# Two early reorderings in the attention stage: the third pair's key rest moves up GpSimd's queue, the fourth pair's copies move behind a reciprocal of the second pair

## The chip, the cores and the metric

One core of a Trainium2 chip runs the whole program in one launch. The metric is the device time of one execution in microseconds (us); a kernel's time is the median of its runs. A profiled execution gives the trace that is read here.

## The reference

Three stages follow each other: causal attention over 2 batches and 12 heads, a dense layer with a squared ReLU, and a layer of 8 experts of which each token takes the best one.

```
scores = q @ k.T / 8                  # seq 448, head_dim 64, causal mask
attn = exp(scores - max) ; attn = attn / (sum(attn) + 1e-9)
x = attn @ v                          # -> [896, 768]
x = relu(x @ w_in)**2 @ w_out         # 768 -> 2048 -> 768
e = argmax(normalised(x) @ normalised(expert_emb).T / tau)
out = gate * (relu(x @ w1[e]) @ w2[e])   # per token, 768 -> 1024 -> 768
```

## The kernel before

Every float32 operand of a product is split into a rounded part (`kh`, `vh`, `pt` high) and the rest (`kl`, `vl`, `pt` low), and three products of the parts make one product. Two heads make a **pair** (`units`, 12 of them; `units[0]` is the first pair here, `units[3]` the fourth). The queries of a pair lie in seven **chunks** of 64, c = 0 to 6; both heads of a chunk fill 128 rows.

For one pair the work is, in this order:

- `s_prep`: the scaled query is rounded on ScalarE (`qs` high) and its rest made on VectorE (`qs` low, line 219). From the third pair on, SyncE then copies it with two DMAs into one of two buffers `q` that TensorE reads (line 230). VectorE rounds the key (`kh`, line 66), and `s_rest` makes its rest (`kl`, line 71) on GpSimd.
- `s_scores`: TensorE makes the scores of a chunk (line 266: high, rest, high), VectorE masks them and finds the maximum (line 276 and a read-out), ScalarE takes the exponential into `p` and sums it (line 279).
- `s_norm`: VectorE makes the reciprocals of the sums (`rs`, line 288), GpSimd multiplies `p` by them (line 292). It is called once for chunks 2, 0, 1, 3 and once for 6, 4, 5.
- `s_trans`: TensorE transposes the probabilities in four groups, **T0 to T3** (line 310, four transposes each). ScalarE rounds a group (`pt` high, line 64), VectorE makes its rest (`pt` low, line 71). T0 needs chunks 0 to 3, T1 chunks 4 to 6. The groups take turns in two PSUM buffers, so T2 waits until VectorE has made T0's rest, T3 waits for T1's, and the next pair's T0 for T2's.
- `s_pv`: TensorE multiplies with v (line 328); the sums go to `xhi` and `xlo`.

The order on TensorE is written out (`products`, `half_unit`): a loop over half pairs k makes scores of one pair, transposes of the pair before it and products with v of the pair before that. On the other engines a scheduler sets the order; `tc.issue_after(x)` and `behind(x)` keep an instruction behind x in it. They put no wait into the program by themselves: on one engine they fix the order in which it works.

Of the kernel before, what the change touches and what calls it, by code (L numbers as in the profile page):

```python
# [13 lines left out]
ALU = mybir.AluOpType  # L14
# [3 lines left out]
B, H, S, D = 2, 12, 448, 64  # L18
# [14 lines left out]
def f32(ap):  # L33
    return ap.bitcast(F32)
# [18 lines left out]
def build(tc, qkd, vd, w_in, w_out, emb, tau, wm, cst, out, dbg_y=None):  # L53
    nc = tc.nc
    V, A, G, T, DMA = nc.vector, nc.scalar, nc.gpsimd, nc.tensor, nc.sync
# [14 lines left out]
    def lo_of(eng, lo, x, hi):  # L70
        return eng.tensor_tensor(out=lo, in0=x, in1=hi, op=ALU.subtract)  # L71
# [63 lines left out]
    last = {}  # L135
# [5 lines left out]
    units = [(b, pr) for b in range(B) for pr in range(NP_)]  # L141
    NU = len(units)
# [6 lines left out]
    maskf = apool.tile([P, S], F32, name="maskf")  # L149
# [19 lines left out]
    def ab(key, u):  # L169
        x = CFG[key]  # L170
        return ENG[x[units.index(u) % len(x)]]
# [24 lines left out]
    def behind(ins):  # L196
        return nullcontext() if ins is None else tc.issue_after(ins.ins)
# [38 lines left out]

    def s_rest(u, eng):
        d = st[u]
        lo_of(eng, d["kl"], d["k"], f32(d["kh"]))

    def s_prep_v(u):
        d = st[u]
# [9 lines left out]
    def s_scores(u, c):  # L252

        d = st[u]
        if "p" not in d:
            for x in ("sm", "mn", "rs"):
                d[x] = apool.tile([P, NQ], F32, tag=x, bufs=3, name=x)
            d["p"] = pz[units.index(u) % len(pz)]
        n = (c + 1) * QC
        ss = ps_s.tile([P, 512], F32, tag="s", name="s")[:, 0:n]  # L260
        first = units.index(u) < CFG["pm"]
        i = COL[c]
        mn = d["mn"][:, i:i + 1]
        order = ((0, "kh"), (1, "kh"), (0, "kl")) if first else ((0, "kh"), (0, "kl"), (1, "kh"))
        for i_, (x, y) in enumerate(order):
            T.matmul(ss, d["q2"][:, c, :, :, x].rearrange("p a b -> p (a b)"), d[y][:, :n],  # L266
                     start=i_ == 0, stop=i_ == 2 and not first)
            if i_ < 2:
                yield
        if first:  # L270

            T.matmul(ss[:, n - QC:n], identb, mask, start=False, stop=True)
            last["max"] = V.reduce_max(out=mn, in_=ss, axis=AX.X, negate=True)
        else:

            last["max"] = V.tensor_tensor_reduce(out=ss, in0=ss, in1=maskf[:, S - n:], scale=-1.0, scalar=3.0e38,  # L276
                                                 op0=ALU.add, op1=ALU.min, accum_out=mn)
        last["max", units.index(u), c] = last["max"]
        last["exp", units.index(u), c] = A.activation(d["p"][c][:, :n], ss, AF.Exp, bias=mn,  # L279
                                                      scale=1.0 if first else -1.0, accum_out=d["sm"][:, i:i + 1])  # L280
        yield
# [95 lines left out]
    def norm_at(k):  # L377
        u = (k + 2) // 2
        if 0 <= u < NU:
            s_norm(units[u], sum(CFG["ch"][k % 2], ()))  # L380
            last["norm", k] = last["norm"]
# [26 lines left out]
    def half_unit(k):  # L408

        u, h = divmod(k, 2)  # L410
        run = {}
        for x in (6, 4, 5) if h == 0 else (2, 0, 1, 3):
            v = u + 1 + h
            if 0 <= v < NU:
                run["s", x] = s_scores(units[v], x)
        if 0 <= u < NU:
            for i in (0, 1) if h == 0 else (2, 3):
                run["t", i] = trans(units[u], i)
        if 1 <= u <= NU:
            for j, g in ((0, 1), (3, 1), (0, 0), (3, 0)) if h == 0 else ((1, 0), (2, 0), (1, 1), (2, 1)):  # L420
                run["v", j, g] = s_pv(units[u - 1], j, g)
        return run
# [56 lines left out]
    def products(k, run):  # L479

        h = k % 2
        if k > 20:
            return last_products(k, run)
        if h == 0:
            mix(run, ("s", 6))
            mix(run, ("t", 0))
            mix(run, ("v", 0, 1), ("v", 3, 1), ("v", 0, 0))
            mix(run, ("s", 4))
            mix(run, ("s", 5))
            mix(run, ("v", 3, 0))  # L490
            if k < 20:
                mix(run, ("t", 1))
            else:
                left.update(run)
        elif k == -3:
            mix(run, *(("s", c) for c in (2, 0, 1, 3)))
        else:
            mix(run, ("t", 2))
            mix(run, ("s", 2))
            mix(run, ("s", 0), ("v", 1, 0))  # L500
            mix(run, ("s", 1), ("v", 2, 0))
            mix(run, ("v", 1, 1))
            mix(run, ("v", 2, 1))
            mix(run, ("t", 3))
            mix(run, ("s", 3))

    for k in range(-3, 2 * NU + 2):
        u, h = divmod(k, 2)
        if k == -2:
            load_v(units[1], last["max", 0, 3])  # L510
            s_load(units[3], last["max", 0, 3])
        elif h == 0:
            if u + 4 < NU:
                with behind(last["q"]):
                    s_load(units[u + 4])
            if u + 2 < NU:
                load_v(units[u + 2])
        if k == 3:
            with tc.issue_after(last["load", 3].ins):
                DMA.dma_start(out=ct, in_=cst)  # L520
        while len(wt) < min(NWI, max(0, (k - CFG["conv0"]) // CFG["convs"])):
            if CFG["pin"]:
                with tc.issue_after(last["max"].ins):
                    w_in_load()
            else:
                w_in_load()
        norm_at(k)
        if k == -1:
            with tc.issue_after(last["norm"].ins):
                s_rest(units[2], ab("kl", units[2]))  # L530
        products(k, half_unit(k))
        if k == -3:
            s_prep(units[1], None, last["max", 0, 3])
            zero_p(1)
            zeros.__exit__(None, None, None)
        if k == 5:
            with behind(last["norm"]):
                G.memset(tri, 1.0)
                G.affine_select(out=tri, in_=tri, pattern=[[1, P]], compare_op=ALU.is_gt, fill=0.0, base=0,
                                channel_multiplier=-1)  # L540
        if k + 3 < len(CFG["wn"]):
            warm(CFG["wn"][k + 3])
        if h == 0 and u + 3 < NU:
            i = u + 1
            s_prep(units[u + 3], last["exp", i, 6 if i else 3], last["max", i, 5], last["max", i, 5], i > 0)
        if h == 1 and 0 <= u + 1 < NU:
            with (tc.issue_after(last["rcp"].ins), tc.issue_after(last["max", 0, 5].ins), tc.issue_after(last["exp", 0, 5].ins),
                  tc.issue_after(last["norm", max(k - 2, 0 if k > 0 else -1)].ins)):
                s_prep_v(units[u + 1])
# [970 lines left out]
```

## Time and profile before

| | us |
|---|---|
| median of 3 runs | 542.58 |
| the runs | 542.92, 542.58, 540.73 |
| profiled execution, its own time | 542.75 |
| its span from first to last instruction | 541.0 |
| TensorE busy in the span | 529.0 |
| VectorE, ScalarE, GpSimd busy | 413.3, 287.4, 201.1 |

The span is cut at the first and the last instruction, so it is 1.75 us shorter than the execution's own time. Times in the rows below count from the span's start. The attention stage lasts from about 5 to about 110 us; the change touches its first quarter.

### The profile page before, as it was taken

What the parts mean: (1) busy time and instruction counts of PE and PEld (TensorE: products, weight loads), DVE (VectorE), ACT (ScalarE), POOL (GpSimd) and SP (SyncE); (2) the same over time, 40 slices, a digit from 0 to 9 for tenths busy, and PEclk for the clock granted to TensorE, in tenths of its full rate; (3) what the DMA queues carried; (4) which work ended last, traced back from release to release, by engine and by line L of the source; (5) the groups of instructions that cost most, each with busy time, mean ns of one, the idle gap of its engine ahead of it and who ended that gap; (6) DMA issues with size and microseconds to landing.
All of it is one profiled execution on the core that took longest, in us unless ns stands there. A gap on an engine that the chain in (4) does not pass through costs nothing.

```text
span 541.0 us, 9614 instructions
## 1 busy us (share of the span) xinstructions
PE 529.0 (98%) x3373; PEld 498.6 (92%) x3374; DVE 413.3 (76%) x979; ACT 287.4 (53%) x635; POOL 201.1 (37%) x270
## 2 busy tenths in 40 slices
PE   8999999999999999999999999999999999999993
PEld 5899999999999999999999989999999999999992
DVE  6989989766786969597899776895296897983741
ACT  6898887333335242433332326631386887764651
POOL 6788989936545643231011201026201301400010
PEclk9999999999999999999999999999999999999998
DMA  4676584333446555358200019304968889884310
GB/s 158 174 184 146 146 238 126 119 115 94 142 138 212 164 186 175 121 174 273 80 30 30 21 31 410 153 2 134 353 210 264 270 278 371 265 277 156 119 53 6
DMA packets 28473, 89.22 MB, mean 165 GB/s; under 512 B 2926, under 2 KB 12270, under 8 KB 28416
## 3 DMA queue, kind: packets, MB, share of 16 engines
q1 hardware_dynamic: 26880, 82.23, 47.6%
q0 software_dynamic: 1536, 6.29, 3.1%
q8 instruction: 28, 0.46, 0.3%
q14 instruction: 29, 0.24, 0.1%
HBM read 78.39 MB, written 6.32 MB: 157 GB/s over the span
## 4 chain that ended last, share of the span: by engine, by line
PE 94%; DVE 3%; POOL 1%; ACT 1%; issue 0%; POOLq 0%; DVEq 0%; ACTq 0%
PE pa L355 22%; PE yps L709 20%; PE ops L1118 11%; PE pv L328 7%; PE s L266 6%; PE pt L310 4%; PE hps L1012 3%; PE ops L1044 3%; PE ops L1049 3%; PE hps L1030 2%; PE hps L1032 2%; PE hps L1031 2%; PE hps L1044 2%; PE hps L1049 2%; PE hps L1013 1%; DVE ml L71 1%
## 5 line engine op out<-in xcount | busy, mean ns | idle before, releaser
L71 DVE TENSOR_TENSOR ml<-xraw,mh 128x768 fp32r<-128x768 f32 x64 | 59.4, 954 | 9.8 <-ACT mh L64 9.4
L64 ACT ACTIVATE mh<-xraw 128x768 fp32r<-128x768 f32 x64 | 52.1, 843 | 7.2 <-PE ops L1044 5.8
L1118 PE MATMUL ops<-mh,act 128*128 128x384 f32 x224 | 53.5, 341 | 0.0
L279 ACT ACTIVATE p<-s,mn 128x192 f32<-128x192 f32 (+6 forms) x84 | 39.9, 478 | 13.8 <-DVE mn L276 7.4
L328 PE MATMUL pv<-pt,v 128*128 128x448 f32 (+7 forms) x288 | 46.2, 295 | 0.0
L266 PE MATMUL s<-kh,q 128*128 128x128 f32 (+6 forms) x168 | 45.6, 323 | 0.2 <-POOL maskf L393 0.2
L292 POOL TENSOR_SCALAR p<-p,rs 128x192 f32<-128x192 f32 (+6 forms) x84 | 43.9, 542 | 3.3 <-DVE rs L288 3.3
L129 DVE SCALAR_TENSOR_TENSOR w<-raw,w 128x768 int32<-128x768 int32 x32 | 42.7, 1338 | 0.7
L328 PEld LDWEIGHTS pv<-pt,v 128*128 128x128 f32 (+1 forms) x288 | 38.5, 163 | 1.9
L1118 PEld LDWEIGHTS ops<-mh,act 128*128 128x128 f32 x224 | 39.2, 188 | 0.8
L1144 POOL DMA_INDIRECT out<-osb,fsi x10 | 10.1, 1013 | 78.4 <-ACT osb L1139 48.8
L71 DVE TENSOR_TENSOR ml<-mraw,mh 128x768 fp32r<-128x768 f32 x32 | 30.1, 955 | 11.3 <-ACT mh L64 10.9
L125 DVE TENSOR_SCALAR w<-raw 128x768 int32<-128x768 int32 x32 | 23.2, 726 | 18.6 <-DMA raw<-in_w_in 4.7
L358 ACT ACTIVATE relu<-pa 128x448 f32<-128x448 f32 x32 | 17.2, 538 | 35.7 <-PE pa L355 35.6
L806 POOL CAST gh<-g 128x1 fp32r<-128x1 f32 x7 | 3.5, 504 | 87.7 <-DVE OHs L800 31.8
L127 DVE SCALAR_TENSOR_TENSOR w<-raw,w 128x768 int32<-128x768 int32 x32 | 35.5, 1113 | 0.7
L71 DVE TENSOR_TENSOR pt<-pt 128x512 fp32r<-128x512 f32 x48 | 32.6, 683 | 2.0 <-ACT pt L64 1.9
L266 PEld LDWEIGHTS s<-kh,q 128*128 128x128 f32 x168 | 31.7, 208 | 2.5 <-POOL maskf L393 1.0
L276 DVE CUSTOM_DVE_ANT_0 s<-s,maskf 128x192 f32<-128x192 f32 (+6 forms) x77 | 31.9, 429 | 2.6 <-PE s L266 2.4
L64 ACT ACTIVATE hs<-h 128x512 fp32r<-128x512 f32 (+1 forms) x32 | 17.7, 573 | 29.5 <-PE yps L709 27.5
L64 ACT ACTIVATE pt<-pt 128x512 fp32r<-128x512 f32 x48 | 28.3, 601 | 7.0 <-PE pt L310 7.0
L71 DVE TENSOR_TENSOR hs<-h,hs 128x512 fp32r<-128x512 f32 (+1 forms) x32 | 21.9, 689 | 13.1 <-ACT hs L64 12.9
(472 smaller groups left out, 1681.2 us busy)
## 6 DMA issues: line engine op xcount, KB each, us to landing
xraw<-in_wm SPq DMA_DIRECT2D x32, 768.0 KB, 5.5
raw<-in_w_in SPq DMA_DIRECT2D x16, 768.0 KB, 4.2
raw<-in_w_out SPq DMA_DIRECT2D x16, 768.0 KB, 4.3
mraw<-in_wm SPq DMA_DIRECT2D x16, 768.0 KB, 8.4
qk<-in_qkd SPq DMA_DIRECT2D x11, 448.0 KB, 4.7
q<-qs SPq DMA_DIRECT2D x20, 224.0 KB, 4.7
v<-in_vd SPq DMA_DIRECT2D x12, 256.0 KB, 5.1
eb<-edram SPq DMA_DIRECT2D x8, 384.0 KB, 4.4
```

Of the source, the lines that this page charges most:

```text
L64: return A.activation(out, in_, AF.Copy, scale=scale)
L71: return eng.tensor_tensor(out=lo, in0=x, in1=hi, op=ALU.subtract)
L127: V.scalar_tensor_tensor(out=w[:, x], in0=raw[:, x, 1], scalar=-0x40000000, in1=w[:, x], op0=ALU.bitwise_and, op1=ALU.bitwise_or)
L129: V.scalar_tensor_tensor(out=w[:, x], in0=raw[:, x, 0], scalar=29, in1=w[:, x], op0=ALU.logical_shift_right, op1=ALU.bitwise_or)
L266: T.matmul(ss, d["q2"][:, c, :, :, x].rearrange("p a b -> p (a b)"), d[y][:, :n], start=i_ == 0, stop=i_ == 2 and not first)
L276: last["max"] = V.tensor_tensor_reduce(out=ss, in0=ss, in1=maskf[:, S - n:], scale=-1.0, scalar=3.0e38, op0=ALU.add, op1=ALU.min, accum_ou ...
L279: last["exp", units.index(u), c] = A.activation(d["p"][c][:, :n], ss, AF.Exp, bias=mn, scale=1.0 if first else -1.0, accum_out=d["sm"][:, ...
L292: last["norm"] = G.tensor_scalar(out=p, in0=p, scalar1=rs[:, COL[c]:COL[c] + 1], scalar2=1.0, op0=ALU.mult, op1=ALU.mult)
L328: T.matmul(d["pv"][:, j * P:S] if h else d["pv"][0:D, j * P:S], d[x][:, j, 1:3].rearrange("p a b -> p (a b)") if h else d[x][:, j, 0], pt[ ...
L355: T.matmul(ps, w[:, kc * P:(kc + 1) * P], x[:, kc, gs], start=n == 1, stop=n == 3 * KC)
L709: T.matmul(ps[t][c][:, :384], x, w[:, c * 384:(c + 1) * 384], start=(f == 0 and w is wh and x is hi), stop=(f == NF - 1 and x is lo))
L1118: T.matmul(ps[c], x, ww[:, col[c]], start=(fc == 0 and x is hh and ww is wh), stop=(fc == 7 and x is hl))
```

## The change

Four edits. At k = -1 the second normalisation of the first pair (chunks 6, 4, 5) is kept behind the third pair's `kl` on GpSimd, where `kl` was behind it or free. The maximum of the second pair's chunk 3 is kept behind the reciprocal of that normalisation on VectorE. The fourth pair's `s_prep` is called at k = 1 in place of k = 0, its rounded query behind the exponential of the second pair's chunk 5, its query rest and rounded key behind the second pair's second reciprocal. The fourth pair's `kl` is kept behind the second pair's last normalisation on GpSimd.

```diff
     def s_rest(u, eng):
         d = st[u]
-        lo_of(eng, d["kl"], d["k"], f32(d["kh"]))
+        last["kl"] = lo_of(eng, d["kl"], d["k"], f32(d["kh"]))
...
-            last["max"] = V.tensor_tensor_reduce(out=ss, in0=ss, in1=maskf[:, S - n:], scale=-1.0, scalar=3.0e38,
-                                                 op0=ALU.add, op1=ALU.min, accum_out=mn)
+            with behind(last["rcp"] if (units.index(u), c) == (1, 3) else None):
+                last["max"] = V.tensor_tensor_reduce(out=ss, in0=ss, in1=maskf[:, S - n:], scale=-1.0, scalar=3.0e38,
+                                                     op0=ALU.add, op1=ALU.min, accum_out=mn)
...
-        norm_at(k)
         if k == -1:
             with tc.issue_after(last["norm"].ins):
                 s_rest(units[2], ab("kl", units[2]))
+            with tc.issue_after(last["kl"].ins):
+                norm_at(k)
+        else:
+            norm_at(k)
...
+        if k == 1:
+            s_prep(units[3], last["exp", 1, 5], last["rcp"], last["rcp"], False)
+            with tc.issue_after(last["norm"].ins):
+                s_rest(units[3], ab("kl", units[3]))
-        if h == 0 and u + 3 < NU:
+        if h == 0 and u + 3 < NU and u != 0:
```

TensorE's own order is the same in both kernels. On the other engines the scheduler's order changes from here to the end of the attention stage; the three places below are the first.

On GpSimd, from the first pair's second normalisation on. `p0c` are the probabilities of the first and third pair, `p1c` of the second; `kl_258` is the third pair's key rest, `kl_347` (afterwards `kl_395`) the fourth pair's, `v10` the second pair's rounded v. Before:

```order
L292 TENSOR_SCALAR p06_121<-p06_121,rs_177 128x448
L292 TENSOR_SCALAR p04_119<-p04_119,rs_177 128x320
L292 TENSOR_SCALAR p05_120<-p05_120,rs_177 128x384
L71 TENSOR_TENSOR kl_258<-qk_155,kh_257 128x448
L292 TENSOR_SCALAR p12_124<-p12_124,rs_273 128x192
L292 TENSOR_SCALAR p10_122<-p10_122,rs_273 128x64
L292 TENSOR_SCALAR p11_123<-p11_123,rs_273 128x128
L292 TENSOR_SCALAR p13_125<-p13_125,rs_273 128x256
L66 CAST v10_113<-v_222 128x4x2x64
L71 TENSOR_TENSOR kl_347<-qk_225,kh_346 128x448
L292 TENSOR_SCALAR p16_128<-p16_128,rs_273 128x448
```

Now:

```order
L71 TENSOR_TENSOR kl_258<-qk_155,kh_257 128x448
L293 TENSOR_SCALAR p06_121<-p06_121,rs_177 128x448
L293 TENSOR_SCALAR p04_119<-p04_119,rs_177 128x320
L293 TENSOR_SCALAR p05_120<-p05_120,rs_177 128x384
L293 TENSOR_SCALAR p12_124<-p12_124,rs_273 128x192
L293 TENSOR_SCALAR p10_122<-p10_122,rs_273 128x64
L293 TENSOR_SCALAR p11_123<-p11_123,rs_273 128x128
L293 TENSOR_SCALAR p13_125<-p13_125,rs_273 128x256
L66 CAST v10_113<-v_222 128x4x2x64
L293 TENSOR_SCALAR p16_128<-p16_128,rs_273 128x448
L293 TENSOR_SCALAR p14_126<-p14_126,rs_273 128x320
L293 TENSOR_SCALAR p15_127<-p15_127,rs_273 128x384
```

The third pair's key rest stands one normalisation earlier; the fourth pair's is gone from this stretch and comes two rows after its end, behind the rest of the second pair's v.

On VectorE, behind the maximum of the second pair's chunk 5. `qs_348` (afterwards `qs_396`) and `kh_346` (`kh_394`) are the fourth pair's, `pt_319<-pt_339` is the rest of the first pair's T1, `pt_361<-pt_362` (afterwards `pt_352<-pt_353`) that of its T2; lines 276 and 277 (an `ISA` row and a read-out) are the maxima of the third pair. Before:

```order
L219 SCALAR_TENSOR_TENSOR qs_348<-qk_225,qs_348 128x448
L66 CAST kh_346<-qk_225 128x448
L276 ISA s_372,mn_370<-s_372,maskf_129 128x192
L276 ISA mn_370 128x1
L71 TENSOR_TENSOR pt_319<-pt_339,pt_318 128x512
L276 ISA s_378,mn_370<-s_378,maskf_129 128x64
L276 ISA mn_370 128x1
L276 ISA s_384,mn_370<-s_384,maskf_129 128x128
L276 ISA mn_370 128x1
L287 TENSOR_SCALAR rs_273<-sm_271 128x3
L71 TENSOR_TENSOR pt_361<-pt_362,pt_360 128x512
L288 RECIPROCAL rs_273<-rs_273 128x3
```

Now:

```order
L71 TENSOR_TENSOR pt_319<-pt_339,pt_318 128x512
L277 ISA s_363,mn_361<-s_363,maskf_129 128x192
L277 ISA mn_361 128x1
L288 TENSOR_SCALAR rs_273<-sm_271 128x3
L277 ISA s_369,mn_361<-s_369,maskf_129 128x64
L277 ISA mn_361 128x1
L277 ISA s_375,mn_361<-s_375,maskf_129 128x128
L277 ISA mn_361 128x1
L289 RECIPROCAL rs_273<-rs_273 128x3
L219 SCALAR_TENSOR_TENSOR qs_396<-qk_225,qs_396 128x448
L66 CAST kh_394<-qk_225 128x448
L71 TENSOR_TENSOR pt_352<-pt_353,pt_351 128x512
```

The fourth pair's two instructions moved from ahead of T1's rest to just ahead of T2's rest, and the reciprocal moved ahead of them.

On ScalarE, at the second pair's exponentials (`p16`, `p14`, `p15`). `pt_318<-pt_339` is the rounded T1 of the first pair, `qs` the fourth pair's rounded query. Before:

```order
L279 ACTIVATE p16_128,sm_271<-s_312,mn_272 128x448
L64 ACTIVATE qs_348<-qk_225 128x448
L279 ACTIVATE p14_126,sm_271<-s_327,mn_272 128x320
L64 ACTIVATE pt_318<-pt_339 128x512
L279 ACTIVATE p15_127,sm_271<-s_333,mn_272 128x384
```

Now:

```order
L280 ACTIVATE p16_128,sm_271<-s_312,mn_272 128x448
L280 ACTIVATE p14_126,sm_271<-s_327,mn_272 128x320
L64 ACTIVATE pt_318<-pt_339 128x512
L280 ACTIVATE p15_127,sm_271<-s_333,mn_272 128x384
L64 ACTIVATE qs_396<-qk_225 128x448
```

The rounded query moved behind the last of the three exponentials and behind T1's rounding.

## Rows read from the trace of the kernel before

**Rows 1.** The page's first part: busy us (share of the span) xinstructions

```profile
PE 529.0 (98%) x3373; PEld 498.6 (92%) x3374; DVE 413.3 (76%) x979; ACT 287.4 (53%) x635; POOL 201.1 (37%) x270
```

**Rows 2.** Busy time by stretch: stretch, us, each engine, clock, DMA share, GB/s

```profile
20.00:30.00 10.00, 9.22 (x76) 8.90 (x75) 9.17 (x34) 8.74 (x29) 8.81 (x16) 1.00 0.62 151
30.00:40.00 10.00, 10.00 (x79) 9.65 (x78) 9.04 (x30) 9.00 (x28) 8.28 (x16) 1.00 0.84 218
```

**Rows 3.** TensorE's waits, 0 to 60 us: us in total, times, longest

```profile
PE pt L310 <- DVE pt L71: 1.0, 2, 0.8
```

**Rows 4.** TensorE's timeline: start, us, instruction, count, [idle before, releaser]

```profile
18.08 0.89 PE L310 MATMUL pt<-ident,p 128*128 128x128 f32 x4
19.19 0.63 PE L310 MATMUL pt<-ident,p 128*128 128x128 f32 x4 [0.21 <-DVE pt L71]
19.57 0.34 PE L266 MATMUL s<-kh,q 128*128 128x192 f32 x1
...
20.55 0.28 PE L266 MATMUL s<-kh,q 128*128 128x128 f32 x1
21.62 0.63 PE L310 MATMUL pt<-ident,p 128*128 128x128 f32 x4 [0.78 <-DVE pt L71]
...
23.06 0.60 PE L310 MATMUL pt<-ident,p 128*128 128x128 f32 x4
...
26.86 0.34 PE L266 MATMUL s<-kh,q 128*128 128x192 f32 x1
...
45.76 0.75 PE L310 MATMUL pt<-ident,p 128*128 128x128 f32 x4
```

**Rows 5.** GpSimd's timeline, 16 to 26 us

```profile
16.38 1.99 POOL L292 TENSOR_SCALAR p<-p,rs 128x448 f32<-128x448 f32 x3 [2.35 <-DVE rs L288]
18.34 1.14 POOL L71 TENSOR_TENSOR kl<-qk,kh 128x448 fp32r<-128x448 f32 x1
19.46 2.10 POOL L292 TENSOR_SCALAR p<-p,rs 128x192 f32<-128x192 f32 x4
...
23.23 1.71 POOL L292 TENSOR_SCALAR p<-p,rs 128x448 f32<-128x448 f32 x3
24.90 1.29 POOL L71 TENSOR_TENSOR v<-v,v 128x512 fp32r<-128x512 f32 x1
```

**Rows 6.** VectorE's timeline, 14 to 23 us

```profile
14.62 0.39 DVE L66 CAST kh<-qk 128x448 fp32r<-128x448 f32 x1
...
16.04 0.17 DVE L288 RECIPROCAL rs<-rs 128x3 f32<-128x3 f32 x1
...
18.36 0.69 DVE L71 TENSOR_TENSOR pt<-pt 128x512 fp32r<-128x512 f32 x1
...
19.43 0.62 DVE L219 SCALAR_TENSOR_TENSOR qs<-qk,qs 128x448 fp32r<-128x448 f32 x1
19.98 0.61 DVE L66 CAST kh<-qk 128x448 fp32r<-128x448 f32 x1
...
20.79 0.68 DVE L71 TENSOR_TENSOR pt<-pt 128x512 fp32r<-128x512 f32 x1
...
22.06 0.68 DVE L71 TENSOR_TENSOR pt<-pt 128x512 fp32r<-128x512 f32 x1
```

**Rows 7.** ScalarE's timeline, 18 to 20 us

```profile
18.40 0.62 ACT L64 ACTIVATE qs<-qk 128x448 fp32r<-128x448 f32 x1
18.91 0.52 ACT L279 ACTIVATE p<-s,mn 128x320 f32<-128x320 f32 x1
...
19.41 0.60 ACT L64 ACTIVATE pt<-pt 128x512 fp32r<-128x512 f32 x1
```

**Rows 8.** SyncE's DMA issues: the query copies of the third and the fourth pair

```profile
14.79 1.37 SPq L230 DMA_DIRECT2D q<-qs  x2
...
20.13 1.39 SPq L230 DMA_DIRECT2D q<-qs  x2
```

**Rows 9.** Tile `qs`, 0 to 60 us: count, ns min/median/max, first and last start

```profile
L219 DVE SCALAR_TENSOR_TENSOR qs<-qk,qs x7: 616/624/1449, 14.1 to 57.0; 128x448 fp32r<-128x448 f32 x7
```

## The prediction

> **What bounds the kernel now.** I read the busy times first. TensorE is busy 529.0 of a span of 541.0 us [rows 1], and from 30 us on whole stretches of the attention stage are full, 10.00 of 10 us, at the full granted clock, the 2.4 GHz level [rows 2]. TensorE's instructions stand in the same order in both kernels, so the change can only give or take waits of TensorE. Next I read where it waits: up to 60 us the list shows 1.0 us behind VectorE's `pt` rests, in two waits [rows 3]. In TensorE's timeline [rows 4] they lie ahead of T2 (0.21 us) and T3 (0.78 us) of the first pair. A wait inside a group does not show as idle: T1 at 18.08 us lasts 0.89 us where the undisturbed T0 at 23.06 lasts 0.60, so 0.29 us is stretch. The next disturbed group of this kind that I show is T0 at 45.76, 0.75 us for 0.60. What the touched stretch could give back is thus little: 0.29 + 0.21 us around T1 and T2, and about 0.95 us ahead of T3 (from the last score matmul at 20.55 to T3 at 21.62 are 1.07 us, of which some 0.12 us is the distance of such matmuls). That is 1.45 us, 0.27% of the run, if all of it stays given back.
>
> **The third pair's key rest.** GpSimd was idle for 2.35 us before 16.38, that is from 14.03, waiting for the reciprocal [rows 5]. The rounded key is ready at 14.62 + 0.39 = 15.01 [rows 6], so `kl`, 1.14 us long [rows 5], fits into that gap and ends near 16.2. The reciprocal, at 16.04 before, now precedes one maximum and can start some 0.38 us earlier, at about 15.66 (an estimate: the three maxima around it leave no idle time). It ends at 15.83 with its 0.17 us; before, the normalisation followed its end (16.21) by 0.17, so 16.0 would be possible and `kl`'s end, 16.2, decides. The normalisation of chunks 6, 4, 5 then starts 0.18 us earlier and ends at 18.19 in place of 18.37. T1, which had to wait for it, ends near 18.8 instead of 18.97. But T2 did not wait for T1: it waited for VectorE's rest of T0 (18.36 + 0.69 = 19.05, released at 19.19) [rows 4, 6], and nothing ahead of that rest moves except the reciprocal among the maxima, which keeps the sum. T2 stays at 19.19 and this part gives **0**. The second pair's normalisation comes 1.14 us earlier, but the T0 that needs it ran undisturbed at 23.06 already.
>
> **The rest of T1 moves up.** Before, T1's rest was behind the fourth pair's query rest and rounded key (19.43 to about 20.5) and a maximum, and ran from 20.79 to 21.47; T3 followed at 21.62, 0.15 us later [rows 4, 6]. Now VectorE reaches it at 19.43, and what decides is T1's rounding on ScalarE. That stood at 19.41, behind the fourth pair's rounded query, which took 0.51 us of the queue (18.40 to 18.91) [rows 7]. So it now starts between 18.9 and 19.41; I take 19.1, since the exponential ahead of it needs a maximum that VectorE ends only just behind 18.36. With its 0.60 us the rest starts at 19.7 (bounds 19.5 and 20.04), ends at 20.4, and T3 could go at 20.55; TensorE gets there at 20.67. T3 gains **0.95 us** (0.74 if the rounding stays at 19.41).
>
> **Where that goes.** The next group, the second pair's T0, needs the buffer of T2, hence T2's rest on VectorE. It ran from 22.06 to 22.74, and T0 at 23.06 found it ready [rows 4, 6]. From 19.43 to 22.06 VectorE worked through eight things in 2.63 us: query rest, rounded key, three maxima, T1's rest, the sums' addition. Now it must go through the same ones and a reciprocal (0.17 us alone, about 0.09 in the queue) between the start of T1's rest and the start of T2's: 2.72 us. From 19.7 that makes 22.42; the rest then ends at 23.1, and T0 can start at 23.25 by the same release of 0.15 us. Two of the durations in the 2.63 us look stretched, above all the rounded key with 0.61 us where the third pair's took 0.39 [rows 6]; without that it is 23.0. The bounds: rest of T1 at 19.5 and 0.45 us less stretch (key and addition) give 22.6, and 20.04 gives 23.6. I take 23.15. So T3 runs a microsecond early and TensorE then waits for T2's rest instead: the wait moves by one group. Against 23.06 this is **+0.1 us**, bounds -0.45 and +0.55.
>
> **The fourth pair's copies.** Its query rest now ends about 0.5 us (key 0.4 to 0.6) ahead of T2's rest at 22.42, near 21.9, against 20.05 before. Issue followed by 0.08 us (20.13) [rows 6, 8], so now at 22.0. The third pair's copy was issued at 14.79, and TensorE used it at 19.57 without a wait [rows 4, 8], so 4.78 us from first issue to use is enough: 26.8. TensorE wants it at 26.86, or 0.1 later by the step above. Cost **0**, with almost no margin left by this bound, where there were 2 us. What is queued behind these DMAs on SyncE is the load of a pair needed a whole pair later. `kl` of the fourth pair: reciprocal near 21.3, normalisation about 0.34 us behind it as at 16.04 and 16.38, then 1.71, 1.29 for the rest of v and 1.14 for `kl` itself [rows 5, 6]: 25.8, which is 1 us ahead of its use.
>
> **The order after that.** VectorE, ScalarE and GpSimd keep a changed order up to the end of the stage, with the same instructions. TensorE is full there, so a better order can give back only stretches like that at 45.76 (0.15 us) [rows 4]; a worse one can add such a stretch to each of nine later pairs, up to 9 x 0.15 = 1.4 us. I take **0**.
>
> **A rule weighed.** The fourth pair's query rest took 0.62 us in the median of seven and 1.45 us at most [rows 9]: something can hold it for 0.8 us. The Trainium skill, "SBUF — State Buffer", section "Who interferes with whom", says that VectorE (with two SBUF inputs or in a two-port mode) and GpSimd exclude each other from a shared pair of ports for a whole instruction. The trace agrees in so far as the rounded key took 0.61 us beside GpSimd's four multiplies, and these 2.10 us [rows 5, 6]. By that rule the moved query rest would meet the second pair's second normalisation, which starts just behind the same reciprocal.
>
> **The sum.** The profiled execution took 542.75 us; 0 + 0.1 + 0 + 0 makes 542.85. It stands 0.17 us above the median of the runs, so I predict **542.6 us**: the same time.
>
> **Rivals.**
>
> - The gain stays. If T2's rest is ready by 22.2, T0 of the second pair starts up to 0.95 us early and all later work with it: 541.6; with the stretch of 45.76 gone, 541.5. For it: the stretches in the 2.63 us; against it: VectorE is busy 9.17 of 10 us there [rows 2] and has no idle time to give.
> - The query rest is held. In its new place, beside the second pair's second normalisation on GpSimd, it takes 1.45 instead of 0.62 us [rows 9], and T2's rest, the second pair's T0 and all behind it shift by 0.8 us: 543.4. For it: six of seven took about 0.62, one did not; against it: the rest would start ahead of the normalisation, which trailed the end of its reciprocal by 0.17 us. The rule weighed above speaks for this case.
> - On the slower side: the fourth pair's query lands late. Place: TensorE at 26.9, before the fourth pair's first scores; nothing else can fill in, since its order is fixed. From 4.9 us behind its issue at 22.0 on, every us costs one us; at 5.6 us the time is 543.3. To be slower by over 0.5% it would have to land after 29.6, 7.6 us behind its issue, for which no row speaks.
> - The later order adds its stretches: up to 542.6 + 1.4 = 544.0.
>
> **Chances and range.** Forecast (542.0 to 543.2) 0.55; the gain stays 0.20; the query rest held 0.08; the query late 0.05; later stretches 0.08; something later in the run that I do not see 0.04. A measurement of this kernel tells a change of about 0.5% from none, that is 2.7 us; no case reaches it, so faster has 0.05, slower 0.04, the same 0.91, where the first two hold the unseen and the width of the runs (2.2 us). The range covers the kept gain with the lower of the runs, 540.8, up to the later stretches, 544.0.
>
> **What would show it.** Right: T2 of the first pair at about 19.2, T3 near 20.7 without a wait, a new wait of TensorE for VectorE's `pt` ahead of the second pair's T0, that T0 near 23.1 and the fourth pair's first scores near 26.9; `kl` of the third pair on GpSimd from 15.05. Wrong: T0 at 22.1 to 22.5 (the gain stays), the scores of the fourth pair behind a wait for a DMA, or T0s of later pairs that last well over 0.60 us.

## The result, and the profile after

The changed kernel's median is 543.69 us (8 runs, 543.32 to 545.84) against 541.50 us (8 runs, 540.47 to 542.92) of the kernel before on the same chip: ratio 1.0051, 95% interval 1.0036 to 1.0067 (the quotient of the two medians alone is 1.0040). The time lies inside the predicted range, but "the same" had been forecast, and the changed kernel is slower by 0.5%: a ratio of 1 lies outside the interval. The runs of either kernel lie in two groups some 2 us apart, and the trace ahead of the prediction is one of the upper group, that of the changed kernel one of the lower; so from here on the changed kernel is compared with a second profile of the kernel before, of the lower group (execution 540.59 us, span 538.9).

The changed kernel's page, its stretches, and TensorE's waits up to 60 us (answering to [rows 1 to 3]):

```profile
PE 527.5 (97%) x3374; PEld 496.7 (92%) x3374; DVE 414.2 (76%) x979; ACT 287.4 (53%) x635; POOL 202.8 (37%) x270
```

```profile
20.00:30.00 10.00, 9.58 (x73) 8.82 (x73) 8.80 (x29) 8.77 (x30) 8.51 (x13) 1.00 0.84 185
30.00:40.00 10.00, 10.00 (x80) 9.68 (x80) 9.27 (x30) 8.56 (x27) 8.56 (x19) 1.00 0.63 160
40.00:50.00 10.00, 9.33 (x77) 8.83 (x75) 9.10 (x29) 8.89 (x27) 8.73 (x16) 1.00 0.57 144
```

```profile
PE pt L311 <- POOL p L293: 1.6, 4, 0.7
...
PE pt L311 <- DVE pt L71: 0.2, 1, 0.2
PE s L266 <- ACT p L280: 0.2, 1, 0.2
```

Where the transposes waited only for VectorE's `pt` rests [rows 3], four of their waits are now for GpSimd's probabilities, 1.6 us together. TensorE's timeline of the changed kernel, the first pair's T1, T2 and T3, the second pair's T0, and what stands behind (as [rows 4]):

```profile
16.66 0.33 PE L311 MATMUL pt<-ident,p 128*128 128x128 f32 x1 [0.68 <-POOL p L293]
17.23 0.99 PE L311 MATMUL pt<-ident,p 128*128 128x128 f32 x7 [0.23 <-POOL p L293]
...
19.19 0.66 PE L311 MATMUL pt<-ident,p 128*128 128x128 f32 x4
...
21.52 0.63 PE L311 MATMUL pt<-ident,p 128*128 128x128 f32 x4 [0.23 <-DVE pt L71]
...
25.33 0.34 PE L266 MATMUL s<-kh,q 128*128 128x192 f32 x1
```

```profile
47.80 0.33 PE L311 MATMUL pt<-ident,p 128*128 128x128 f32 x1 [0.43 <-POOL p L293]
48.36 0.98 PE L311 MATMUL pt<-ident,p 128*128 128x128 f32 x7 [0.24 <-POOL p L293]
```

```profile
104.19 0.31 PE L329 MATMUL pv<-pt,v 128*64 128x320 f32 x1
105.51 1.54 PE L329 MATMUL pv<-pt,v 128*64 128x320 f32 x11 [1.01 <-DVE pt L71]
```

TensorE's order is the same in both kernels, so the two traces can be laid over each other matmul by matmul. The **lag** of the changed kernel, that is how much later the same matmul starts than in the second profile of before, at the places where it changes:

```
before   after    lag
 14.37   14.41   +0.04   T0, first pair
 16.13   17.23   +1.10   T1, first pair (waits for GpSimd's p)
 19.31   19.19   -0.12   T3, first pair
 20.75   21.52   +0.76   T0, second pair
 46.69   48.36   +1.67   T1, fifth pair (waits for GpSimd's p)
 54.56   56.09   +1.52
 88.56   90.45   +1.89   scores (wait for ScalarE's p)
102.35  105.51   +3.16   last products with v (wait for VectorE's pt)
  end     end    +3.3    spans 538.9 and 542.2
```

So 0.8 us are lost where the change was made, and 2.5 us further on, at three places: 0.9, 0.4 and 1.3 us (about 0.2 us come back near 55 us). The two traces thus differ by 3.3 us; the ratio of the runs makes it 2.8 us (2.0 to 3.6). Behind the attention stage nothing changes: 436.55 us from that last place to the end before, 436.69 now.

GpSimd, VectorE and SyncE at the first place, of the changed kernel (as [rows 5, 6, 8]):

```profile
13.86 1.62 POOL L71 TENSOR_TENSOR kl<-qk,kh 128x448 fp32r<-128x448 f32 x1
15.46 3.21 POOL L293 TENSOR_SCALAR p<-p,rs 128x448 f32<-128x448 f32 x7
```

```profile
18.44 0.69 DVE L71 TENSOR_TENSOR pt<-pt 128x512 fp32r<-128x512 f32 x1 [1.21 <-ACT pt L64]
...
19.87 0.60 DVE L219 SCALAR_TENSOR_TENSOR qs<-qk,qs 128x448 fp32r<-128x448 f32 x1
20.39 0.39 DVE L66 CAST kh<-qk 128x448 fp32r<-128x448 f32 x1
20.69 0.68 DVE L71 TENSOR_TENSOR pt<-pt 128x512 fp32r<-128x512 f32 x1
```

```profile
20.54 1.28 SPq L230 DMA_DIRECT2D q<-qs  x2
```

T1's rest (18.44) waits for T1, T1 waits for the normalisation (15.46), and that for `kl`.

The second of the three places can be read from the traces at hand: it lies in ScalarE's order near 90 us. Of the kernel before (second profile), then of the changed one, `v` being the rounded v of the last pair; and TensorE's scores of the changed kernel behind it:

```profile
88.00 0.42 ACT L279 ACTIVATE p<-s,mn 128x192 f32<-128x192 f32 x1 [1.04 <-DVE mn L276]
88.41 0.62 ACT L64 ACTIVATE v<-v 128x512 fp32r<-128x512 f32 x1
```

```profile
89.37 0.63 ACT L64 ACTIVATE v<-v 128x512 fp32r<-128x512 f32 x1 [0.94 <-PE pv L329]
89.91 0.40 ACT L280 ACTIVATE p<-s,mn 128x192 f32<-128x192 f32 x1
```

```profile
90.45 0.47 PE L266 MATMUL s<-kh,q 128*128 128x448 f32 x1 [0.21 <-ACT p L280]
```

The rounding of v, which itself waits for TensorE's products, now stands ahead of the exponential, and TensorE's next scores wait for that exponential. In the runs below the lag rises here by 0.3 to 0.4 us wherever ScalarE stands in this order and TensorE reached the place without another loss (six traces, the changed kernel among them), and by at most 0.03 us where the exponential stands first.

### The profile page after: what moved, and what is told of

Its sections match the earlier page's. It is cut to its first block, busy times and chain, and to the rows that moved or that the text cites. A ratio compares the mean times of both kernels' runs of the same rounds, so it can differ in the third digit from the quotient of the medians.

```text
span 542.2 us, 9614 instructions
## 1 busy us (share of the span) xinstructions
PE 527.5 (97%) x3374; PEld 496.7 (92%) x3374; DVE 414.2 (76%) x979; ACT 287.4 (53%) x635; POOL 202.8 (37%) x270
## 4 chain that ended last, share of the span: by engine, by line
PE 87%; DVE 8%; POOL 2%; issue 1%; ACT 1%; DMA 0%; POOLq 0%; SPq 0%; ACTq 0%; DVEq 0%
PE pa L356 21%; PE yps L717 20%; PE ops L1126 11%; PE pv L329 5%; PE s L266 4%; PE hps L1020 3%; PE pt L311 3%; PE ops L1052 3%; PE ops L1057 3%; PE hps L1038 2%; PE hps L1040 2%; PE hps L1039 2%; PE hps L1052 2%; PE hps L1057 2%; PE hps L1021 1%; DVE ml L71 1%
## 5 line engine op out<-in xcount | busy, mean ns | idle before, releaser
L266 PE MATMUL s<-kh,q 128*128 128x128 f32 (+6 forms) x168 | 44.4, 311 | 0.7 <-ACT p L280 0.4
L129 DVE SCALAR_TENSOR_TENSOR w<-raw,w 128x768 int32<-128x768 int32 x32 | 42.9, 1343 | 0.6
L127 DVE SCALAR_TENSOR_TENSOR w<-raw,w 128x768 int32<-128x768 int32 x32 | 37.8, 1184 | 0.7
L266 PEld LDWEIGHTS s<-kh,q 128*128 128x128 f32 x168 | 30.6, 199 | 3.3 <-ACT p L280 1.4
```

What stands on the lines that cost most here:

```text
L127: V.scalar_tensor_tensor(out=w[:, x], in0=raw[:, x, 1], scalar=-0x40000000, in1=w[:, x], op0=ALU.bitwise_and, op1=ALU.bitwise_or)
L129: V.scalar_tensor_tensor(out=w[:, x], in0=raw[:, x, 0], scalar=29, in1=w[:, x], op0=ALU.logical_shift_right, op1=ALU.bitwise_or)
```

## The experiments

The theory after the result, **later order**: the early edits cost under 1 us, and the rest comes from places where the scheduler's order, changed up to the end of the stage, puts something ahead of an instruction that TensorE waits for. Two rivals: the early wait makes the later ones (**passed on**), or one held instruction near 95 us does (**port hold**). The ratios are against runs of the kernel before on the same chip; the runs were made on several chips, so it is the ratios that can be compared. Edits are shown without their helper lines, which "..." stands for.

**The kernel before once more**, for a second profile.

> The kernel before once more, for a second trace of it. Both kernels' runs fall into two groups about 2 us apart (before 540.5 to 541.0 and 542.0 to 542.9, after 543.3 to 543.9 and 545.4 to 545.8), and the two traces at hand differ by 3 us in TensorE's place already at 13.3 us, ahead of any edit. Theory (the change costs about 2.8 us in either group): if this run is of the quick group, about 540.6, TensorE reaches the first pair's T1 near 15.8 as in the changed kernel, and shows no waits near 47.8 and 104.7. Rival (the changed kernel's trace was only luckier at the start): TensorE's place at 13.3 us is the same as in the first trace of before whatever the time.

Measured: 540.59 us, and TensorE reaches T1 at 15.79 us, as the theory has it. GpSimd, behind the first four multiplies of the first pair:

```profile
11.63 2.22 POOL L292 TENSOR_SCALAR p<-p,rs 128x192 f32<-128x192 f32 x4
14.08 1.99 POOL L292 TENSOR_SCALAR p<-p,rs 128x448 f32<-128x448 f32 x3 [0.23 <-DVE rs L288]
16.03 1.16 POOL L71 TENSOR_TENSOR kl<-qk,kh 128x448 fp32r<-128x448 f32 x1
```

The idle time of 2.35 us into which the prediction put `kl` [rows 5] is 0.23 us here. It belongs to executions with the late start of the first trace: of all the profiles below, only one starts as late, and it alone has a gap of that size again (2.28 us, in the second of the three tries at the end).

**Half the change: the key rest and the maximum**, without the fourth pair's move.

```diff
-            s_prep(units[3], last["exp", 1, 5], last["rcp"], last["rcp"], False)   # at k == 1
...
-        if h == 0 and u + 3 < NU and u != 0:
+        if h == 0 and u + 3 < NU:
```

> The key rest ahead of the normalisation and the maximum behind the reciprocal, without the moved fourth pair. GpSimd's order from the fifth pair on is here mostly that of the changed kernel (v's rest ahead of a pair's second normalisation; v's rest ahead of the first weight's cast). Theory (the later order costs the 2.8 us, by the waits near 48 and 105): about 1.5 to 2.8 us over before, with TensorE waits for GpSimd's p between 40 and 60 us and for VectorE's pt rest near 105. Rival (the moved fourth pair costs it, at 13 to 27 us): within 0.5 us of before.

Measured: 543.50 us, ratio 1.0061 (1.0041 to 1.0081). The loss near 90 us and the wait of 1.0 us ahead of the last products with v are there. The one at the fifth pair's T1, which the theory expected too, is not; in its place 0.5 us are lost near 62 us.

**The other half: the fourth pair's move alone** (the edit against the changed kernel).

```diff
-            with tc.issue_after(last["kl"].ins):
-                norm_at(k)            # k == -1: the key rest behind the normalisation again
...
-            with behind(last["rcp"] if (units.index(u), c) == (1, 3) else None):
```

> The moved fourth pair alone. GpSimd's order from the fifth pair on is here that of before but for one pair of rows. Theory (the later order costs): within 0.7 us of before, 540.6 in the quick group, no wait near 48 and 105. Rival (the moved fourth pair costs it): 2 to 3 us over before.

Measured: 541.66 us (12 runs, 540.12 to 544.66), ratio 1.0028 (1.0007 to 1.0048), profiled at 540.99 us. GpSimd keeps, in the later pairs, the order of the kernel before, and from 21 us to the end of the stage the lag stays near 0.6 us: none of the three later losses. (The medians make it 1.3 us, 0.4 to 2.6 by the interval; the rival, 2 to 3 us, does not show in the trace.) T3 and T0 of TensorE, and VectorE between them:

```profile
18.38 0.63 PE L310 MATMUL pt<-ident,p 128*128 128x128 f32 x4
...
21.29 0.63 PE L310 MATMUL pt<-ident,p 128*128 128x128 f32 x4 [0.99 <-DVE pt L71]
```

```profile
18.27 0.99 DVE L287 TENSOR_SCALAR rs<-sm 128x3 f32<-128x3 f32 x1
...
20.47 0.68 DVE L71 TENSOR_TENSOR pt<-pt 128x512 fp32r<-128x512 f32 x1
```

T3 comes 0.93 us earlier (19.31 before), T0 0.54 us later (20.75): the wait moved on by one group, as forecast. The first row of VectorE, which adds a constant to three sums per partition, took 0.99 us and ended at 19.26, 0.03 us behind the end of GpSimd's work beside it (a rounding of v, 18.63 to 19.23).

**The changed kernel, the second weight's steps one maximum earlier on VectorE.** Its first step had taken 2.21 us near 95 us, beside GpSimd's rest of the first weight, and 0.56 us in the kernel before: the port hold.

```diff
-                with tc.issue_after(last["max"].ins):
+                with tc.issue_after((last["max", NU - 1, 4] if len(wt) == 1 else last["max"]).ins):
                     w_in_load()
```

> The changed kernel with one VectorE instruction (the first step of the second weight, line 125) one maximum earlier, so that it starts ahead of GpSimd's rest of the first weight and not just behind its start; in the changed kernel it took 2.21 us there. Theory (GpSimd's two-input operation holds VectorE's instruction, and TensorE's 1.0 us wait at 104.2 is its late end): the instruction takes under 1.0 us, the wait at 104.2 goes, the time is about 1.0 us under the changed kernel, 1.8 over before. Rival (VectorE is simply behind by its load): the wait stays at 0.5 us or more and the time within 0.3 us of the changed kernel.

Measured: 543.62 us, ratio 1.0071 (1.0049 to 1.0093). The first step takes 0.55 us now and the next one 2.42; the last wait is 0.93 us. So the hold was moved to the next step and not taken away, and this run alone doesn't part it from the wait. The run after the next one does: there the first step takes 2.19 us again, and the wait is gone.

**The early edit undone, the later order kept.** GpSimd's key rest stands behind the normalisation again; the maximum and the fourth pair stay moved. GpSimd's early order is that of the fourth pair's move alone; VectorE's and ScalarE's order, and GpSimd's behind 25 us, are those of the changed kernel.

```diff
-            with tc.issue_after(last["kl"].ins):
-                norm_at(k)
+            norm_at(k)                # ahead of s_rest(units[2], ...), as before
```

> The changed kernel with its first edit undone: on GpSimd the third pair's key rest stands behind the first pair's second normalisation again. The first 25 us of GpSimd's, VectorE's and ScalarE's order are then those of the run that made the fourth pair's part alone (profiled at 540.99 us), and GpSimd's order behind them is that of the changed kernel, rests of v ahead of normalisations. Theory, the later order costs by itself: TensorE's wait for GpSimd ahead of T1 (0.68 and 0.23 us near 16 us) is gone, T3 comes early, the second pair's T0 waits as in the run of the fourth pair's part (0.5 us of lag), and behind it the three losses of the changed kernel stand again, 0.9 near 47 us, 0.4 near 89 us and 1.2 near 104 us: 540.99 + 2.5 = 543.5 us for a profile of the same start. Rival, the early wait on GpSimd makes the later ones: 541.0 us, as that run.

Measured: 543.72 us, ratio 1.0062 (1.0039 to 1.0085), profiled at 543.53. TensorE's timeline:

```profile
19.11 0.62 PE L311 MATMUL pt<-ident,p 128*128 128x128 f32 x4
...
47.74 0.33 PE L311 MATMUL pt<-ident,p 128*128 128x128 f32 x1 [0.42 <-POOL p L293]
48.30 0.88 PE L311 MATMUL pt<-ident,p 128*128 128x128 f32 x6 [0.23 <-POOL p L293]
...
105.37 1.55 PE L329 MATMUL pv<-pt,v 128*64 128x320 f32 x11 [1.01 <-DVE pt L71]
```

No wait at T1 of the first pair any more, T3 early (-0.20, from a start that lagged by 0.87), and all three later losses to within 0.1 us (0.9, 0.4, 1.2). With the early waits on GpSimd gone and the losses kept, "passed on" falls: the later order makes them. (T0 still lags by 0.74 us here; that such a lag alone makes no later loss is shown by the last run below, 1.3 us late at T0 in the old order and no later from there on.)

**The last pair's rest of v behind its last normalisation.** A single place of GpSimd's order, as in the kernel before.

```diff
-        lo_of(V if u == units[0] and CFG["u0"] else ab("vl", u), vl, v, f32(vh))
+        with behind(last["norm"] if u == units[-1] else None):
+            lo_of(V if u == units[0] and CFG["u0"] else ab("vl", u), vl, v, f32(vh))
```

> The changed kernel, with one edit that touches the order of GpSimd at one place alone: the rest of the last pair's v is kept behind that pair's last normalisation. Theory, the later order: the last step of the second weight's loading on VectorE (1.93 us, beside that rest) takes 0.96 us as in the kernel before, the last wait (1.01 us) goes, the waits near 48 us stay: 543.6 - 1.2 = 542.4 us. Rival, the normalisation that now stands beside that step holds it as long, or the hold of 2.21 us ten microseconds earlier decides: 543.5 us.

Measured: 542.43 us (12 runs), ratio 1.0038 (1.0019 to 1.0057). VectorE of the changed kernel, then of this one; line 129 is the last step of the third weight (not of the second, as the expectation says), behind it the `pt` rest that the last products need:

```profile
102.92 1.93 DVE L129 SCALAR_TENSOR_TENSOR w<-raw,w 128x768 int32<-128x768 int32 x1
104.78 0.68 DVE L71 TENSOR_TENSOR pt<-pt 128x512 fp32r<-128x512 f32 x1
```

```profile
102.74 0.96 DVE L129 SCALAR_TENSOR_TENSOR w<-raw,w 128x768 int32<-128x768 int32 x1
103.62 0.68 DVE L71 TENSOR_TENSOR pt<-pt 128x512 fp32r<-128x512 f32 x1
```

```profile
102.04 1.99 POOL L71 TENSOR_TENSOR v<-v,v 128x512 fp32r<-128x512 f32 x1
```

The last row is the changed kernel's GpSimd: its subtraction for v, 1.29 us long elsewhere, ran into the steps of VectorE. With it out of the way the step takes 0.96 us, the wait is gone, and the lag falls by 1.0 us there; elsewhere the two traces agree to within 0.2 us. On GpSimd that subtraction is the only instruction in another place, and VectorE's and ScalarE's order is the same up to the end of the stage, so this place is settled. The step near 95 us still takes 2.19 us: "port hold" there falls.

**The fifth pair's rest of v behind its second normalisation.**

```diff
...
+        with behind(last["norm"] if u == units[4] else None):
```

> The changed kernel, with one edit: on GpSimd the rest of the fifth pair's v is kept behind that pair's second normalisation. From there on the scheduler also puts the last pair's rest of v behind its last normalisation again. Theory, the later order: TensorE's waits for the fifth pair's probabilities (0.43 and 0.24 us near 48 us) and for VectorE's pt ahead of the last pair's products with v (1.01 us near 105 us) go, and with them 0.9 and 1.2 us of lag: 543.6 - 2.1 = 541.5 us, the loss in the first 23 us (0.8 us) and the one near 90 us (0.4 us) stay. Rival, the loss is made in the first 23 us and the later waits only pass it on: 543.5 us. Rival, the second weight's first step beside GpSimd's rest of the first weight (2.21 us, near 95 us) makes the last wait: that order is the same in so far as the weight's rest still comes first, so only 0.9 us go, 542.7 us.

Measured: 543.32 us (9 runs), ratio 1.0045 (1.0028 to 1.0062): the theory's 541.5 was missed by 1.8 us. The last wait went, but the fifth pair's T1 still waits (0.23 us, at 48.46). GpSimd there:

```profile
46.38 0.22 POOL L289 TENSOR_SCALAR rs<-sm 128x4 f32<-128x4 f32 x1 [1.12 <-ACT p L281]
46.69 1.71 POOL L294 TENSOR_SCALAR p<-p,rs 128x448 f32<-128x448 f32 x3
```

The fifth pair's multiplies start at 46.69, no earlier than in the changed kernel (46.58): GpSimd now stands idle for 1.12 us in place of working on the rest of v, since the addition for the next pair's sums, which waits for ScalarE, still stands ahead of them. So the rest of v is not what holds T1. The loss of 0.5 us in place of 0.9 comes from TensorE, which was 0.5 us later already. And the new order brought a new wait: near 88 us VectorE works through all three steps of the first weight (1.23, 1.06 and 0.96 us) ahead of a `pt` rest, and TensorE loses 1.26 us.

**The fifth pair's second sums ahead of its first multiplies**, with the last pair's rest of v behind as above. From the third pair on GpSimd makes the additions ahead of the reciprocals. The one for chunks 6, 4, 5 stood ahead of the first four multiplies in the kernel before (40.82, then 42.27 us), behind them in the changed one (44.56, behind 42.94).

```diff
...
+        if k == 6:
+            s_norm(units[u], sum(CFG["ch"][0], ()), "rcp")      # addition and reciprocal alone
+        if k == 7:
...
+            s_norm(units[u], cs, "add")
+            with tc.issue_after(last["add"].ins):
+                s_norm(units[u], sum(CFG["ch"][0], ()), "mul")  # the first multiplies, behind it
...
```

> The changed kernel with the last pair's rest of v behind its last normalisation (as in the run with that edit alone, 542.4 us) and, for the fifth pair, the addition of the second three sums ahead of the first four multiplies on GpSimd, as it stood before the change (40.82 us, ahead of 42.27). Theory: the wait near 48 us comes from this addition, which stood behind the four multiplies (44.56 us), and the reciprocal behind it: 542.4 - 0.9 = 541.5 us, without a wait of TensorE for GpSimd's p near 47 us. Rival: the rest of v between the addition and the multiplies makes it: 542.4 us and the wait stays.

Measured: 542.30 us (12 runs, 540.75 to 544.71), ratio 1.0028 (1.0011 to 1.0045), profiled at 541.75. GpSimd and TensorE at the fifth pair:

```profile
43.06 0.24 POOL L290 TENSOR_SCALAR rs<-sm 128x3 f32<-128x3 f32 x1
43.40 3.25 POOL L301 TENSOR_SCALAR p<-p,rs 128x192 f32<-128x192 f32 x7
```

```profile
47.66 1.09 PE L319 MATMUL pt<-ident,p 128*128 128x128 f32 x8
```

The seven multiplies run through and T1 doesn't wait. Of TensorE's lag behind the changed kernel 1.0 us goes there; but 0.4 us has come up just ahead of it, at T0, which waits inside the group (1.03 us long, 0.60 in the changed kernel), since the first multiplies now end later. That leaves 0.6 us, where the theory had 0.9. Near 105 us 1.2 us more go, and since ScalarE's exponential stands ahead of the rounding of v again, the loss near 90 us doesn't come either: behind 30 us the lag behind the kernel before grows by 0.3 us in all, where it grows by 2.4 in the changed kernel. The medians of this run and of the one with the last pair's rest of v alone differ by 0.1 us and their ratios by 0.5 us, less than the intervals can tell. The edit also took the rest of v and the next pair's addition from between: it shows that this stretch of GpSimd's order makes the wait, and not which of its instructions does.

**Three tries for a faster order.** Query rest behind T1's rest, rounded key behind T2's rest, without and with the rests of v of the fifth and the last pair behind the normalisations; and, in the kernel before, the rounded key alone behind T1's rest.

```diff
...
+            s_prep(units[3], last["pth", 0, 1], last["ptl", 0, 1], last["ptl", 0, 2], False)
...
```

```diff
-            s_prep(units[u + 3], last["exp", i, 6 if i else 3], last["max", i, 5], last["max", i, 5], i > 0)
+            s_prep(units[u + 3], last["exp", i, 6 if i else 3], last["max", i, 5],
+                   last["ptl", 0, 1] if u == 0 else last["max", i, 5], i > 0)
```

> The kernel before, with the fourth pair's copies moved in another way: the rounded query behind the rounding of the first pair's T1, the query rest behind T1's rest, the rounded key behind T2's rest, and the fourth pair's key rest behind the second pair's last normalisation, the rest of the second pair's v behind that. T3 of the first pair comes 0.93 us earlier, as where the fourth pair's part was made alone. Theory, what that run lost again at the second pair's T0 (1.26 us) was T2's rest behind query rest, rounded key and reciprocal: here T2's rest stands ahead of the key and the reciprocal and about 0.7 us of the gain stay. Its later order is that of the changed kernel, rests of v ahead of normalisations, which costs 0.9 us near 48 us and 1.2 us near 105 us: 540.4 - 0.7 + 2.1 = 541.8 us. Rival, the later order costs nothing by itself: 539.7 us. Rival, the gain is lost at T0 again: 540.7 or 542.8 us.

> As the run before (copies split), and on GpSimd the rests of the fifth and the last pair's v kept behind the normalisations. Theory, the later order: 540.4 - 0.7 = 539.7 us, faster than both kernels. Rival, the later order costs nothing by itself: the same time as the run before. Rival, the gain is lost at the second pair's T0: 540.7 us.

> The kernel before with one edit: on VectorE the fourth pair's rounded key, and nothing else of it, stands behind the rest of the first pair's T1. GpSimd's order is that of the kernel before to the end. Theory: T1's rest starts 0.5 us earlier and T3 with it, T2's rest ahead of the second pair's T0 has the same work ahead of it, so that T0 comes 0.1 to 0.3 us earlier at most, and with the later order kept nothing is lost behind: 540.4 - 0.2 = 540.2 us, the same time as before within what a run can tell. Rival, T1's rest or the key is held beside GpSimd's multiplies (by up to 0.8 us): 541.2 us.

Measured: 544.36 us (ratio 1.0058, 1.0037 to 1.0080), 545.80 us (1.0075, 1.0053 to 1.0097) and 541.67 us (1.0012, 0.9999 to 1.0025). All three missed; in the first and the third what their rivals say came: an instruction held beside GpSimd, and the gain lost at T0. VectorE of the first of them, then of the third:

```profile
18.24 1.46 DVE L219 SCALAR_TENSOR_TENSOR qs<-qk,qs 128x448 fp32r<-128x448 f32 x1
```

```profile
18.80 1.19 DVE L66 CAST kh<-qk 128x448 fp32r<-128x448 f32 x1
...
20.30 0.99 DVE L287 TENSOR_SCALAR rs<-sm 128x3 f32<-128x3 f32 x1
21.21 0.68 DVE L71 TENSOR_TENSOR pt<-pt 128x512 fp32r<-128x512 f32 x1
```

The moved query rest took 1.46 us in place of 0.63, the moved key 1.19 (0.62 before) and the addition behind it 0.99, all beside GpSimd's work, and the gain at T3 (0.95 and 0.28 us) was lost again at the second pair's T0 (20.91 and 22.03 us, 20.75 before). Behind it the first lost 1.4 us more up to 33 us, and then 1.0, 0.4 and 1.2 us at the three places of the changed kernel: the later order's price once more. The second gave the last of these back, and had no loss of 0.4 us, but lost 0.8 us near 60, where TensorE waits for a query copy, and 1.3 us near 94 us: keeping two instructions behind moved the losses instead of ending them. In the third, with the old order kept on GpSimd, the lag of 1.3 us at T0 stays as it is up to the end. No version here beat the kernel before.

## Why the prediction was wrong

The sum of the forecast was +0.1 us; the trace shows +3.3, of which 0.8 in the touched stretch and 2.5 behind it. That the time still lies inside the range is luck: the forecast stood on a median of three runs, 542.58, where the eight runs of the kernel before have 541.50; from there its upper bound of +1.4 us would have ended at 542.9.

- **The third pair's key rest, forecast 0.** Against the fourth pair's move alone the whole change has T0 of the second pair 0.23 us later (21.52 and 21.29), so the size nearly held, but the working didn't: `kl` did not fit into GpSimd's gap, since that gap is 0.23 us in an execution with the quicker start. (Whether it fits into the gap of 2.35 us no run shows: the changed kernel has no trace with the late start.) It pushed the normalisation from 14.08 to 15.46 us and T1 into two waits (0.68 and 0.23 us). Of these 0.9 us only 0.2 reach T0, because T0 waits for T2's rest, and that came 0.22 us later (20.69 and 20.47).
- **The rest of T1 moves up, forecast 0.95 us at T3.** Right where the key rest didn't disturb it: 0.93 us with the fourth pair's move alone. In the whole change T1's late start leaves 0.12.
- **Where that goes, forecast +0.1 us at the second pair's T0, bounds -0.45 and +0.55.** Right mechanism, mis-sized: +0.54 alone and +0.76 in the whole change. In the one run the addition of the sums, part of the 2.63 us of the working (seven things, not eight), took 0.99 us beside GpSimd; in the whole change it took 0.16, but T1's delay ran through VectorE's queue to T2's rest.
- **The fourth pair's copies, forecast 0.** Right: issued at 20.54, used at 25.33, 4.79 us later and without a wait.
- **The order after that, forecast 0, at most 9 x 0.15 = 1.4 us.** This step failed. It cost 2.5 us in the trace (0.9, 0.4 and 1.3), shown by the run that undid the early edit and kept the losses, and, for the first and the last place, by edits there: the wait near 48 us went (0.6 us net), and so did the one near 105 us (1.0 us). The bound was taken from a stretch that TensorE already had, 0.15 us [rows 4]. That stretch did go (T0 of the fifth pair lasts 0.60 us in the changed kernel), and the wait came behind it. A changed order doesn't repeat existing stretches: it can put any instruction ahead of one that TensorE waits for, here the next pair's addition, among others, on GpSimd, the rounding of v on ScalarE and, near the end of the stage, a subtraction that stretches a weight step on VectorE to 1.93 us. The 0.4 us near 90 us are read from ScalarE's order in the traces; no edit was made for them alone.
- **The rivals.** "The later order adds its stretches" (0.08, 544.0) was the one that came, with waits in place of stretches. "The query rest is held" did not come in the changed kernel (0.60 us at 19.87) but in the run with the copies split (1.46 us). "The gain stays" did not come, with T0 0.76 us later, nor "the query is late", with no wait at 25.33.
- **Slips in the sums.** 542.85 less 0.17 is 542.68, put down as 542.6; and the lower end of the range, 540.8, does not hold the kept gain with the lowest run, which is 540.73 - 0.95 = 539.8. Neither bears on the verdict.

The Trainium skill, "SBUF — State Buffer", section "Who interferes with whom", says that a VectorE instruction with two SBUF inputs contends with a GpSimd instruction that reads SBUF, and that whoever issues first keeps the shared ports for its whole instruction and the other blocks. The runs agree: line 129, with two inputs in SBUF, took 1.93 us beside GpSimd's subtraction, which started ahead of it, and 0.96 without it. The section also names the forms that need those ports, so the last of the three losses could have been looked for by it: at each place where the order of VectorE or GpSimd changes, the pair of instructions that now meet. The other two are read above from the order of a queue alone.

## What to carry to other kernels

Where a scheduler sets the order, an edit at one place can be an edit of everything behind it: lay the orders side by side to the end, and look ahead of each instruction that the busy engine waits for, at what now stands there and how long the longest of it can take. Price a new wait by that, not by waits that are there already. A gap on an idle engine read from one trace may belong to that execution: a second profile of the same kernel would have shown 0.23 us where the first showed 2.35.

## What was not expected of the hardware

An addition on three sums per partition took 0.99 us on VectorE beside GpSimd's work in two runs, and 0.16 us in the changed kernel (19.32 us). In the two runs it ended at 19.26 and 21.29 us, 0.02 to 0.03 us behind the end of GpSimd's instruction beside it (19.23 and 21.27). So in these two runs a small instruction kept VectorE's queue until the other engine's was done.

The two profiles of the kernel before differ before the first instruction that the change touches: the matmul that starts at 13.3 us in the second starts 2.2 us later in the first, and the spans differ by 2.1 us. Matmuls of the same kind, in the first profile of the kernel before and in the second; 448 columns take 1.31 us for two in the one and 0.68 us in the other:

```profile
9.60 1.31 PE L266 MATMUL s<-kh,q 128*128 128x448 f32 x2
```

```profile
8.38 0.68 PE L266 MATMUL s<-kh,q 128*128 128x448 f32 x2
```

And the stretch from 8 to 11 us of the two (columns as in [rows 2]):

```profile
8.00:11.00 3.00, 3.00 (x11) 1.89 (x10) 2.69 (x10) 2.23 (x9) 0.00 (x0) 1.00 0.29 117
```

```profile
8.00:11.00 3.00, 3.00 (x18) 1.92 (x16) 2.94 (x11) 2.10 (x10) 0.83 (x1) 1.00 0.23 93
```

The granted clock reads 1.00, the 2.4 GHz level, in both, with 11 and 18 matmuls in the stretch. Why the one is half as quick stays open.
